# Pooled attention and a softplus feed-forward layer: two head pairs' attention results in one PSUM buffer, and the weights' combinations begun at the fifth chunk

## The chip, the cores and the metric

The kernel runs on one core of a Trainium2 chip. The metric is the device time of one execution in microseconds (us). The kernel before took 983.45 us (median of three runs, 981.61 to 985.9). Engines are named as the profile names them: PE is the matrix engine (PEld its weight loads), DVE is VectorE, ACT is ScalarE, POOL is GpSimd, SP is SyncE, which issues most of the DMAs.

## The reference

```python
# q, k, v: (8, 8, 576, 64) float32; w_in (512, 2048), w_out (2048, 512)
def _attn_ref(q, k, v):
    B, H, S, D = q.shape
    pool = 8
    Sp = S // pool                                   # 72 pooled keys
    k_p = k.reshape(B, H, Sp, pool, D).mean(axis=3)
    v_p = v.reshape(B, H, Sp, pool, D).mean(axis=3)
    scores = (1.0 / np.sqrt(D)) * np.matmul(q, k_p.transpose(0, 1, 3, 2))
    scores = scores - np.max(scores, axis=-1, keepdims=True)
    attn = np.exp(scores)
    attn = attn / (np.sum(attn, axis=-1, keepdims=True) + 1e-09)
    return np.matmul(attn, v_p)

def _moe_ref(x, w_in, w_out):                        # x: (4608, 512), the attention's output
    h = x @ w_in
    g = np.maximum(h, 0.0) + np.log1p(np.exp(-np.abs(h)))
    return g @ w_out
```

## The kernel before

**Chunks.** The 4608 tokens are cut into 18 chunks of 256 (two tiles of 128), numbered from 0. A batch has 576 tokens, so a chunk lies in one batch or spans two. For each chunk the kernel computes the attention, which gives the chunk's input x (512 wide, transposed, four head pairs m of 128 rows), then the first products (x with w_in), the softplus g, and the second products (g with w_out).

**High and low parts.** Every fp32 operand is split into a part rounded to the matmul's format and the rest of it, and a product is made of three matmuls: high with high, high with low, low with high. So each result that comes out of PSUM and goes into another matmul is read twice: ScalarE casts the high part, and VectorE subtracts it from the PSUM value for the low part. For the attention's result these two are `av_high` (line 500) and `av_low` (line 503), for the probabilities `PT_high` (432) and `PT_low` (437), for g `pair_softplus` (571) and `pair_low` (577).

**Two phases.** Chunks 0 to 2 and the attention of chunk 3 run in a first phase, while the weights are unpacked. All the rest is the second phase. There the first and second products go in pairs of feed-forward blocks, `u` = 0 to 7 for each chunk: `pair1` (24 matmuls of 256 columns, line 520) and, up to chunk 5, `pair2` (12 matmuls of 512, line 590). From chunk 6 on, `pair2_fast` (line 683) makes the second products with seven block products instead of eight, 21 matmuls of 256 columns. For that it needs sums of blocks of g (`sums`, `sums_high`, `sums_low`, lines 609, 614, 619) and combinations of blocks of w_out.

**The combinations of the weights** (`combine`, line 645; `combined_high`, 650; `combined_low`, 654; `put_t`, 658; `load_t`, 662) are made once, for each u: eight VectorE steps on 256 or 512 columns in two parts, and for each part a ScalarE cast, a VectorE subtraction and a store of 512 KB to DRAM. After chunk 5's products have released the weights that lie in their place, four loads of 256 KB for each u bring them back. They hold one of three `ld` buffers, which the loads of keys and values use too, and one of two `S` buffers per part.

**The order of the second phase** is a list made by a planner in the kernel's source (`Order`). Each operation has an engine, an estimated cost, the operations it waits for, and the buffers (`Slot`s) it holds. The planner walks through time; of the operations that an engine could start within 0.4 us of the earliest one, it takes the one with the highest rank (the estimated length of the work that hangs on it) plus a bonus `first`. `HURRY` is 60, `EARLY` is 100. The list fixes each engine's order; on the chip an engine takes its instructions in that order and waits where an input is late. Keys and values of the next batches go through SP (loads) and POOL (sums over eight rows).

**PSUM.** It has eight banks of 512 columns. In the second phase two are for first products, four for sums of second products, and two (`bank`) are for everything in the attention: transposes of q, scores, transposes of the probabilities, and the attention's results `avp`.

**Attention one chunk ahead.** In the stage of chunk c the attention of chunk c+1 goes on: transposes of q (`qTp`, 352), scores (365), their minimum and difference (373, 381), one exponential for the whole chunk (316) that waits for the third pair's softplus, sums and normalisation (396 to 412), transposes of the probabilities (`ptp`, 427, and `ltp`, 443), and at last `av_products` (497), for each head pair four matmuls of up to 256 columns for each batch in the chunk. Each head pair has a bank of its own turn: four matmuls (eight where the chunk spans two batches), one ACT cast and one DVE subtraction of 256 columns, and then the bank is free. The transposes of q for chunk c+2 need `av_products` of chunk c+1 and one of the two banks. The first step of first products of chunk c+1 is cut into 18 matmuls that need head pairs 0 to 2 and 6 that need head pair 3.

**Outputs.** Up to chunk 5, `output` copies the two sums out of their banks (ACT line 549, DVE line 551) with `HURRY`; later chunks are put together in `finish` (696, 704). The stores (`put`, 555) have no bonus and nothing hangs on them.

Of the kernel before, what the change touches and what calls it, by code (L numbers as in the profile page):

```python
# [9 lines left out]
F32 = mybir.dt.float32  # L10
# [84 lines left out]
def pooled_attention_softplus_ffn(  # L95
# [41 lines left out]
    def turn(banks, name):  # L137

        banks.append(banks.pop(0))
        return psum.tile([P, 512], F32, tag=banks[-1], name=name)  # L140
# [355 lines left out]
                                        (vsh[i][:, m], pl[:, m]), (vlo[i][:, m], lt[:, m // 2]))):  # L496
                nc.tensor.matmul(out=ps[:, r], lhsT=w, rhs=x[:, r], start=j == 0, stop=j == 3)  # L497

    def av_high(c, m, ps):
        nc.scalar.copy(out=pt_[c][0][:, m], in_=ps[:, 0:CT])  # L500

    def av_low(c, m, ps):
        nc.vector.tensor_tensor(out=pt_[c][1][:, m], in0=ps[:, 0:CT],  # L503
                                in1=pt_[c][0][:, m].bitcast(F32), op=ALU.subtract)

    def av(c, m):
        ps = turn(at_banks, "avp")
        av_products(c, m, ps)
        av_high(c, m, ps)
        av_low(c, m, ps)  # L510


    gs, accs = {}, {}
# [208 lines left out]
    def bank(s, name):  # L722
        if s.tile is None:
            s.tile = psum.tile([P, 512], F32, tag=s.name, name=name)
        return s.tile

    def act(n):
        return 0.14 + 0.00094 * n
# [447 lines left out]
    def probabilities(c, tiles, s_E, s_lt, subs):  # L1176
        s_x, norms, lows = x_slot[c], [], []
        parts = lambda n, k: [o for b in sorted({b for _, _, b in n}) for o in k.get(b, ())]
        ex = op(ACT, 1.2 + 2 * 1.28, lambda: exponential(e_[c]), [*subs, third[c - 1]], [s_E])
        for x in tiles:  # L1180
            s_sm, s_pm, s_pe = Slot("sm"), Slot("pm"), Slot("pe")
            o = op(DVE, 0.76, x.sum, [ex], [s_E, s_sm])
            o = op(DVE, 0.38, x.reciprocal, [o], [s_sm])
            m = op(DVE, 0.7, lambda x=x: x.main(nc.vector), [o], [s_E, s_sm, s_pm])
            e = op(DVE, 0.52, x.ends, [o], [s_E, s_sm, s_pe])
            s, r = Slot("bank"), Slot("bank")
            o = op(PE, 0.45, lambda x=x, s=s: x.PT(bank(s, "ptp")), [m], [s, s_pm], first=EARLY)
            h = op(ACT, act(512), lambda x=x, s=s: x.PT_high(s.tile), [o], [s, s_x])
            lows.append(op(DVE, dve2(512), lambda x=x, s=s: x.PT_low(s.tile), [h], [s, s_x]))
            o = op(PE, 0.15, lambda x=x, r=r: x.last(bank(r, "ltp")), [e], [r, s_pe], first=EARLY)  # L1190
            h = op(ACT, act(256), lambda x=x, r=r: x.last_high(r.tile), [o, h], [r, s_lt])
            lows.append(op(DVE, dve2(256), lambda x=x, r=r: x.last_low(r.tile), [h], [r, s_lt]))
        sp = spans(c * CT, (c + 1) * CT)
        for m in range(HP):
            s = Slot("bank")
            o = op(PE, 0.47 if len(sp) == 1 else 0.9,
                   lambda m=m, s=s: av_products(c, m, bank(s, "avp")),
                   [*lows, *parts(sp, v_ready)], [s, s_lt, s_x], first=EARLY)
            av_done[c].append(o)
            o = op(ACT, act(CT), lambda m=m, s=s: av_high(c, m, s.tile), [o], [s, s_x])  # L1200
            x_done[c].append(op(DVE, dve2(CT), lambda m=m, s=s: av_low(c, m, s.tile), [o],
                                [s, s_x]))

    def first_products(c, u, before):
# [7 lines left out]
        if u == 0:  # L1212
            wait += x_done[c] or [None]
        if u == 0:
            o = op(PE, 18 * MM, lambda: pair1(c, u, bank(s, "h"), range(KC - 1)), wait[:-1],
                   [s, x_slot[c]])
            o = p1[c, u] = op(PE, 6 * MM, lambda: pair1(c, u, s.tile, range(KC - 1, KC)),
                              [o, wait[-1]], [s, x_slot[c]])
        else:
            o = p1[c, u] = op(PE, 24 * MM, lambda: pair1(c, u, bank(s, "h")), wait,  # L1220
                              [s, x_slot[c]])
# [50 lines left out]
    def output(c, ends, banks):  # L1272
        s_o = [Slot("o") for _ in range(T)]
        if len(ends) > 1:
            s_u = Slot("u")
            o = op(ACT, 0.4, lambda: finish(c, 0), ends[:1], [*s_o, s_u, banks[0]], first=HURRY)
            i = op(DVE, 1.27, lambda: finish(c, 1), [o], [*s_o, s_u, *banks[:2]], first=HURRY)
            o = op(DVE, 1.7, lambda: finish(c, 2), [i, ends[1]], [*s_o, s_u, *banks[2:]],
                   first=HURRY)
            drained[c] = i, o  # L1280
            copies = [o] * T
        else:
            out_[c] = {}

            def copy(t):
                out_[c][t] = copy_out(c, t)
            copies = [op(DVE if t % 2 else ACT, 0.68, lambda t=t: copy(t), ends,
                         [s_o[t], banks[t]], first=HURRY) for t in range(T)]
        for t in range(T):
            op(SYNC, 1.0, lambda t=t: put(c, t, out_[c][t]), [copies[t]], [s_o[t]], lag=2.2)  # L1290

    def combinations():
        for u in range(FP):
            s_d, last, t_ready[u] = Slot("ld"), None, []
            for part in range(2):
                for step in range(4):
                    last = op(DVE, 0.7 if part == step == 0 else 0.43,
# [71 lines left out]
```

## Time and profile before

| | us |
|---|---|
| median of three runs | 983.45 |
| the profiled execution | 983.81 |
| its span, first to last instruction | 982.1 |
| PE busy | 942.4 |
| DVE busy | 669.0 |
| ACT busy | 420.6 |
| POOL busy | 117.6 |

The profile is of one execution. The granted PE clock over the whole span is 0.99 of full speed. Busy PE time is modelled and PE's instructions overlap; times of PE's wait rows (in square brackets behind an instruction, with what ended the wait) are idle time. The second phase begins at about 200 us; the stage of chunk 4 begins at 264.20 us, that of chunk 5 at 322.03, that of chunk 6 at 375.11, and from there on a stage takes about 51 us. The combinations run from 155.3 to 280.5 us, their reloads are issued from 324.6 to 380.1 us.

### The profile page before, as it was taken

What the parts mean: (1) busy time and instruction counts of PE and PEld (TensorE: products, weight loads), DVE (VectorE), ACT (ScalarE), POOL (GpSimd) and SP (SyncE); (2) the same over time, 40 slices, a digit from 0 to 9 for tenths busy, and PEclk for the clock granted to TensorE, in tenths of its full rate; (3) what the DMA queues carried; (4) which work ended last, traced back from release to release, by engine and by line L of the source; (5) the groups of instructions that cost most, each with busy time, mean ns of one, the idle gap of its engine ahead of it and who ended that gap; (6) DMA issues with size and microseconds to landing.
All of it is one profiled execution on the core that took longest, in us unless ns stands there. A gap on an engine that the chain in (4) does not pass through costs nothing.

```text
span 982.1 us, 18423 instructions
## 1 busy us (share of the span) xinstructions
PE 942.4 (96%) x7232; PEld 894.8 (91%) x7232; DVE 669.0 (68%) x1496; ACT 420.6 (43%) x854; POOL 117.6 (12%) x149
## 2 busy tenths in 40 slices
PE   5889999999899999999999999999999999999998
PEld 4679998898788899999999999999999999999997
DVE  5899987579874235767676766677757666666654
ACT  4763333444443333435353435353445343444332
POOL 1000001023342221042003300013200000000000
PEclk9999999999799999999999999999999999999999
DMA  9846343145262687578667847486747564755562
GB/s 252 262 154 236 126 153 139 58 157 179 78 208 55 183 251 248 188 227 240 185 196 202 260 146 224 151 241 193 244 140 236 162 214 153 214 173 194 172 213 88
DMA packets 105383, 181.56 MB, mean 185 GB/s; under 512 B 45648, under 2 KB 59984, under 8 KB 105296
## 3 DMA queue, kind: packets, MB, share of 16 engines
q1 hardware_dynamic: 103216, 179.86, 59.5%
q8 instruction: 57, 0.93, 0.4%
q10 hardware_dynamic: 2080, 0.52, 0.3%
q14 instruction: 30, 0.25, 0.1%
HBM read 154.14 MB, written 26.21 MB: 184 GB/s over the span
## 4 chain that ended last, share of the span: by engine, by line
PE 82%; DVE 11%; ACT 3%; DMA 2%; issue 1%; SPq 0%; DVEq 0%; ACTq 0%
PE h L520 38%; PE m L683 22%; PE acc L543 6%; PE acc L590 5%; PE sc L365 4%; PE avp L497 3%; PE qTp L352 2%; DVE sf L609 1%; PE ptp L427 1%; DVE d L645 1%; DVE t L654 1%; DVE xl L503 1%; DMA q<-in_q_dram 1%; ACT g L571 1%; DVE so L619 1%
## 5 line engine op out<-in xcount | busy, mean ns | idle before, releaser
L520 PE MATMUL h<-xh,w 128*128 128x256 f32 x2304 | 422.8, 284 | 2.4 <-DVE w L817 1.2
L520 PEld LDWEIGHTS h<-xh,w 128*128 128x128 f32 x2304 | 356.8, 189 | 6.7 <-DVE w L817 1.7
L520 PE MATMUL h<-xl,w 128*128 128x256 f32 x1152 | 324.6, 282 | 0.0
L571 ACT ACTIVATE g<-h 128x512 f32<-128x512 f32 x240 | 130.5, 596 | 292.5 <-PE h L520 278.3
L520 PEld LDWEIGHTS h<-xl,w 128*128 128x128 f32 x1152 | 217.4, 189 | 0.0
L683 PE MATMUL m<-w,so 128*128 128x256 f32 x1152 | 154.2, 282 | 0.0
L683 PEld LDWEIGHTS m<-w,so 128*128 128x128 f32 x1152 | 144.0, 188 | 0.0
L609 DVE TENSOR_TENSOR sf<-g 128x128 f32<-128x128 f32 x192 | 59.2, 308 | 119.5 <-ACT g L571 119.0
L683 PE MATMUL m<-w,g 128*128 128x256 f32 x576 | 113.4, 286 | 0.0
L577 DVE TENSOR_TENSOR gl<-g 128x512 fp32r<-128x512 f32 x120 | 85.6, 713 | 28.0 <-ACT g L571 28.0
L205 POOL TENSOR_TENSOR kst<-kst 72x512 f32<-72x512 f32 (+1 forms) x48 | 52.1, 1086 | 386.4 <-DMA kst<-in_k_dram 215.9
L683 PEld LDWEIGHTS m<-w,g 128*128 128x128 f32 x576 | 87.9, 188 | 0.0
L614 ACT CAST so<-sf 128x512 fp32r<-128x512 f32 x96 | 59.6, 621 | 57.5 <-DVE sf L609 57.5
L683 PE MATMUL m<-w,gl 128*128 128x256 f32 x288 | 80.9, 281 | 0.0
L619 DVE TENSOR_TENSOR so<-sf,so 128x512 fp32r<-128x512 f32 x96 | 69.3, 721 | 8.5 <-ACT so L614 1.6
L590 PE MATMUL acc<-w,g 128*128 128x512 f32 x192 | 63.0, 410 | 0.0
L373 DVE TENSOR_REDUCE mn<-sc 128x4 f32<-128x288 f32 x72 | 32.0, 453 | 42.5 <-PE sc L365 42.0
L543 PE MATMUL acc<-w,g 128*128 128x512 f32 x192 | 60.6, 396 | 0.3 <-ACT g L526 0.3
L526 ACT ACTIVATE g<-h 128x256 fp32r<-128x256 f32 (+1 forms) x96 | 31.9, 383 | 56.5 <-PE h L520 44.6
L683 PEld LDWEIGHTS m<-w,gl 128*128 128x128 f32 x288 | 54.2, 188 | 0.2 <-DVE gl L577 0.2
L365 PE MATMUL sc<-kbd,qT 128*128 128x144 f32 (+1 forms) x320 | 46.1, 297 | 1.9 <-DVE kbd L223 1.0
L365 PEld LDWEIGHTS sc<-kbd,qT 128*128 128x128 f32 (+1 forms) x320 | 38.8, 182 | 6.4 <-issue 1.7
(176 smaller groups left out, 1256.6 us busy)
## 6 DMA issues: line engine op xcount, KB each, us to landing
w<-wi SPq DMA_DIRECT2D x192, 512.0 KB
out_dram<-o SPq DMA_DIRECT2D x36, 256.0 KB
wst<-in_moe_w_in_dram SPq DMA_DIRECT2D x16, 512.0 KB
wst<-in_moe_w_out_dram SPq DMA_DIRECT2D x16, 512.0 KB
wi<-w SPq DMA_DIRECT2D x16, 512.0 KB
t<-t SPq DMA_DIRECT2D x16, 512.0 KB
w<-t SPq DMA_DIRECT2D x32, 256.0 KB
q<-in_q_dram SPq DMA_DIRECT2D x30, 256.0 KB
```

The source lines that it names most:

```text
L205: nc.gpsimd.tensor_tensor(out=out, in0=x, in1=y, op=ALU.add)
L365: nc.tensor.matmul(out=ps[r, (m % 2) * 2 * SP:(m % 2 + 1) * 2 * SP], lhsT=self.q[:, m, r], rhs=kbd[b % 2][:, m, :], start=True, stop=True)
L373: nc.vector.tensor_reduce(out=self.mn[:, 4 * i:4 * i + 4], in_=self.view(ps), axis=AX.X, op=ALU.min)
L520: nc.tensor.matmul(out=ps[:, 0:CT], lhsT=w[:, kc * P:(kc + 1) * P], rhs=x[:, kc], start=first and kc == j == 0, stop=last and kc == KC - 1 ...
L543: nc.tensor.matmul(out=accs[c][t], lhsT=a[:, ts], rhs=w, start=f == 0 and j == 0, stop=f == FC - 1 and j == 2)
L571: nc.scalar.activation(out=g, in_=ps.rearrange("p (k i) -> p k i", k=2), func=AF.Softplus)
L577: nc.vector.tensor_tensor(out=gl, in0=g, in1=gh.bitcast(F32), op=ALU.subtract)
L590: nc.tensor.matmul(out=accs[c][t], lhsT=a[:, k, ts], rhs=w, start=u == 0 and k == 0 and j == 0, stop=u == FP - 1 and k == 1 and j == 2)
L609: nc.vector.tensor_tensor(out=sf[:, o], in0=x, in1=y, op=how)
L614: nc.scalar.copy(out=so[:, 0], in_=ss[c, u])
L619: nc.vector.tensor_tensor(out=so[:, 1], in0=sf, in1=so[:, 0].bitcast(F32), op=ALU.subtract)
L683: nc.tensor.matmul(out=ms[c][n], lhsT=x, rhs=y, start=u == 0 and j == 0 and n in (1, 6, 5, 4), stop=u == FP - 1 and j == 2 and n in (2, 7, ...
```

## The change

Three things are changed, all in the second phase.

- The attention's results of two head pairs go into one bank, 256 columns each. They are one operation on PE, with estimated cost 0.94 (1.8 where the chunk spans two batches), and then one ACT cast and one DVE subtraction of 512 columns. The first step of a chunk's first products is cut in two halves of 12 matmuls: the first needs the first two head pairs, the second the other two.
- The first operation of each u's combinations waits for the first step of first products of chunk 4, `p1[NF - 2, 0]`, the fifth chunk; before, it waited for nothing.
- The copies of the sums of chunks 2 to 5, and all output stores, have a bonus of 2000 in place of 60 and 0.

```diff
-    def av_high(c, m, ps):
-        nc.scalar.copy(out=pt_[c][0][:, m], in_=ps[:, 0:CT])
-
-    def av_low(c, m, ps):
-        nc.vector.tensor_tensor(out=pt_[c][1][:, m], in0=ps[:, 0:CT],
-                                in1=pt_[c][0][:, m].bitcast(F32), op=ALU.subtract)
...
+    def av_high(c, m, ps, n=1):
+        nc.scalar.copy(out=pt_[c][0][:, m:m + n],
+                       in_=ps[:, 0:n * CT].rearrange("p (n i) -> p n i", n=n))
+
+    def av_low(c, m, ps, n=1):
+        nc.vector.tensor_tensor(out=pt_[c][1][:, m:m + n],
+                                in0=ps[:, 0:n * CT].rearrange("p (n i) -> p n i", n=n),
+                                in1=pt_[c][0][:, m:m + n].bitcast(F32), op=ALU.subtract)
...
-        for m in range(HP):
+        for m in range(0, HP, 2):
             s = Slot("bank")
-            o = op(PE, 0.47 if len(sp) == 1 else 0.9,
-                   lambda m=m, s=s: av_products(c, m, bank(s, "avp")),
-                   [*lows, *parts(sp, v_ready)], [s, s_lt, s_x], first=EARLY)
+
+            def products(m=m, s=s):
+                ps = bank(s, "avp")
+                for n in range(2):
+                    av_products(c, m + n, ps[:, n * CT:(n + 1) * CT])
+            o = op(PE, 0.94 if len(sp) == 1 else 1.8, products, [*lows, *parts(sp, v_ready)],
+                   [s, s_lt, s_x], first=EARLY)
             av_done[c].append(o)
-            o = op(ACT, act(CT), lambda m=m, s=s: av_high(c, m, s.tile), [o], [s, s_x])
-            x_done[c].append(op(DVE, dve2(CT), lambda m=m, s=s: av_low(c, m, s.tile), [o],
+            o = op(ACT, act(512), lambda m=m, s=s: av_high(c, m, s.tile, 2), [o], [s, s_x])
+            x_done[c].append(op(DVE, dve2(512), lambda m=m, s=s: av_low(c, m, s.tile, 2), [o],
                                 [s, s_x]))
...
-            o = op(PE, 18 * MM, lambda: pair1(c, u, bank(s, "h"), range(KC - 1)), wait[:-1],
+            o = op(PE, 12 * MM, lambda: pair1(c, u, bank(s, "h"), range(KC // 2)), wait[:-1],
                    [s, x_slot[c]])
-            o = p1[c, u] = op(PE, 6 * MM, lambda: pair1(c, u, s.tile, range(KC - 1, KC)),
+            o = p1[c, u] = op(PE, 12 * MM, lambda: pair1(c, u, s.tile, range(KC // 2, KC)),
                               [o, wait[-1]], [s, x_slot[c]])
...
-                         [s_o[t], banks[t]], first=HURRY) for t in range(T)]
+                         [s_o[t], banks[t]], first=2000) for t in range(T)]
         for t in range(T):
-            op(SYNC, 1.0, lambda t=t: put(c, t, out_[c][t]), [copies[t]], [s_o[t]], lag=2.2)
+            op(SYNC, 1.0, lambda t=t: put(c, t, out_[c][t]), [copies[t]], [s_o[t]], lag=2.2,
+               first=2000)
 
     def combinations():
         for u in range(FP):
-            s_d, last, t_ready[u] = Slot("ld"), None, []
+            s_d, last, t_ready[u] = Slot("ld"), p1[NF - 2, 0], []
```

More of the change, by code (lines that the diff above doesn't have):

```diff
@@ L497, in av_products @@
                 nc.tensor.matmul(out=ps[:, r], lhsT=w, rhs=x[:, r], start=j == 0, stop=j == 3)
-    def av_high(c, m, ps):
-        nc.scalar.copy(out=pt_[c][0][:, m], in_=ps[:, 0:CT])
-    def av_low(c, m, ps):
-        nc.vector.tensor_tensor(out=pt_[c][1][:, m], in0=ps[:, 0:CT],
-                                in1=pt_[c][0][:, m].bitcast(F32), op=ALU.subtract)
[L506 to L510, printed above, removed]
+    def av_high(c, m, ps, n=1):
[5 more added lines that the diff above has]
+                                in1=pt_[c][0][:, m:m + n].bitcast(F32), op=ALU.subtract)
     gs, accs = {}, {}
```

## The prediction

> **What bounds the kernel now.** I read the page first: busy times, then the chain of work that ended last.
>
> ```profile
> span 982.1 us, 18423 instructions
> ...
> PE 942.4 (96%) x7232; PEld 894.8 (91%) x7232; DVE 669.0 (68%) x1496; ACT 420.6 (43%) x854; POOL 117.6 (12%) x149
> ...
> PE 82%; DVE 11%; ACT 3%; DMA 2%; issue 1%; SPq 0%; DVEq 0%; ACTq 0%
> ```
>
> PE is busy for 96% and carries 82% of the chain; VectorE carries 11%. So work taken off VectorE or ScalarE pays only where PE stands idle for it. The change touches two such places: the stages in which the weights' combinations run, and the chunk boundaries, where the attention result of the next chunk is copied out of PSUM.
>
> For the first place I cut the time at the starts of first products (chunk 3, pair 1; chunk 4; chunk 5; chunk 6) and asked for busy time in these windows. The columns are the window, its length, PE, PE weight load, DVE, ACT and POOL busy with counts, granted clock, DMA share and GB/s.
>
> ```profile
> 206.19:264.20 58.01, 52.55 (x330) 46.92 (x329) 55.75 (x101) 25.08 (x45) 20.75 (x21) 0.93 0.46 151
> 264.20:322.03 57.83, 56.25 (x375) 50.43 (x374) 36.34 (x69) 22.26 (x40) 22.25 (x25) 0.98 0.41 119
> 322.03:375.11 53.08, 53.05 (x358) 48.62 (x358) 17.90 (x39) 17.89 (x32) 9.55 (x12) 1.00 0.79 232
> ```
>
> In the stage of chunk 3 VectorE is busy 55.75 of 58.01 us: there it is the bound, and PE is idle 58.01 - 52.55 = 5.46 us and runs at a granted clock of 0.93, which costs about 0.07 x 52.55 = 3.68 us. The stage of chunk 4 has 1.58 us of idle PE and 0.02 x 56.25 = 1.13 us of clock; the stage of chunk 5 has 0.03 us. The same windows for the combinations alone (tile d with its rounded tables t; columns DVE, ACT, clock, DMA share, GB/s), and PE's rows around the worst wait:
>
> ```profile
> 150.00:206.19 56.19, 4.24 (x9) 0.83 (x2) 1.00 0.27 91
> 206.19:264.20 58.01, 34.46 (x57) 7.15 (x12) 0.93 0.46 151
> 264.20:322.03 57.83, 8.68 (x15) 1.86 (x3) 0.98 0.41 119
> ```
>
> ```profile
> 250.79 1.12 PE L427 MATMUL ptp<-ident,pm 128*128 128x128 f32 x4 [3.31 <-DVE pm L405]
> ...
> 257.83 0.39 PE L443 MATMUL ltp<-ident,pe 128*96 128x128 f32 x2 [0.34 <-DVE lt__2751 L452]
> 258.89 0.33 PE L497 MATMUL avp<-xh,vsh 128*128 128x128 f32 x1 [0.67 <-DVE xl L437]
> ```
>
> ```profile
> 252.34 4.72 PE acc L590 x12
> ...
> 270.29 2.77 PE acc L590 x12
> ```
>
> Of VectorE's 55.75 us, 34.46 are combinations. The attention of chunk 4 is queued among them, its probabilities come late, PE waits 3.31 us, and twelve products just after take 4.72 us where twelve later ones take 2.77: the clock fell with that wait.
>
> For the second place, the waits of the whole run grouped by who waited for whom (us, times, longest):
>
> ```profile
> PE avp L497 <- DVE xl L503: 4.9, 9, 1.5
> ...
> PE ptp L427 <- DVE pm L405: 4.1, 2, 3.3
> ...
> PE qTp L352 <- DVE xl L503: 3.1, 7, 0.5
> ...
> PE ltp L443 <- DVE xl L437: 1.2, 2, 0.8
> ```
>
> The first and third, 8.0 us, are PE waiting until the low part of an attention result has been copied, so that one of the two attention banks comes free. One boundary in order of time:
>
> ```profile
> 467.94 0.28 PE L497 MATMUL avp<-xh,vsh 128*128 128x256 f32 x1
> ...
> 468.90 0.40 PE L683 MATMUL m<-w,g 128*128 128x256 f32 x2
> ...
> 469.11 0.65 ACT L500 CAST xh<-avp 128x256 fp32r<-128x256 f32 x2
> ...
> 471.34 0.76 DVE L503 TENSOR_TENSOR xl<-avp,xh 128x256 fp32r<-128x256 f32 x2
> 471.82 0.38 PE L497 MATMUL avp<-xh,vsh 128*128 128x256 f32 x1 [0.27 <-DVE xl L503]
> ...
> 473.48 1.14 PE L352 MATMUL qTp<-ident,q 128*128 128x128 f32 x8 [0.44 <-DVE xl L503]
> ...
> 474.37 0.48 PE L520 MATMUL h<-xh,w 128*128 128x256 f32 x2
> ```
>
> Head pairs 0 and 1 are multiplied from 467.94, then a step of second products fills in, and pairs 2 and 3 wait for the banks, then the next q transposes wait again; the first products of the new chunk start at 474.37.
>
> **The merge of two head pairs.** Fourteen chunks (4 to 17) go this way. Four ACT casts and four DVE subtractions of 256 columns become two each of 512. The old ones have their own groups; for the new ones the nearest are the copies of the probabilities, of the same kind and size:
>
> ```profile
> L503 DVE TENSOR_TENSOR xl<-avp,xh 128x256 fp32r<-128x256 f32 x72 | 28.8, 421 | 21.2 <-ACT xh L500 19.7
> L500 ACT CAST xh<-avp 128x256 fp32r<-128x256 f32 x72 | 25.9, 380 | 41.7 <-PE avp L497 40.2
> ...
> L437 DVE TENSOR_TENSOR xl<-ptp,xh 128x512 fp32r<-128x512 f32 x36 | 24.7, 687 | 3.9 <-ACT xh L432 3.4
> ...
> L432 ACT CAST xh<-ptp 128x512 fp32r<-128x512 f32 x36 | 21.3, 590 | 14.7 <-PE ptp L427 14.7
> ```
>
> Per chunk ACT saves 4 x 0.380 - 2 x 0.590 = 0.34 us and DVE 4 x 0.421 - 2 x 0.687 = 0.31, which by itself is off the path. What counts is the banks: two couples fit the two attention banks, so all four head pairs can be multiplied back to back (1.92 us, twice the 0.96 from 467.94 to 468.90), then the 2.5 us of second products run, and meanwhile both couples are copied. At the boundary shown, second products would end at 467.94 + 1.92 + 2.5 = 472.4. DVE is free for the couples at 471.34, as now: first low part done at 472.0, second at 472.7. The q transposes (0.89 us, 473.48 to 474.37) start at 472.4 and the first products at about 473.3 instead of 474.37. That is the 0.71 us of waits and a little more. Of the 8.0 us I take 6.0, since the second q transpose needs the second bank and where DVE is late some wait remains. Bounds: -8.0 and 0 (the list could keep the present order, and then the banks are reached no earlier).
>
> Two steps from the chain of waits give the size of what PE does in between, one of second and one of first products:
>
> ```profile
> 484.77 2.49 PE m L683 x21
> 487.26 2.84 PE h L520 x24
> ```
>
> The first part of a chunk's first step becomes 12 products instead of 18, about 12/24 x 2.84 = 1.42 us. The second couple's copy ends 0.69 us after the first, so that part hides it; with the cover gone it would cost 0.69 per chunk.
>
> [...] The trace shows the ACT copy at 469.11, behind both head pairs already, because softplus stands before it; by the row the sum keeps its -6.0.
>
> **The combinations begin with chunk 4.** Moved as one body: 64 DVE steps, 16 ACT casts, 16 DVE subtractions, 16 stores of 512 KB on SP; the 32 reloads of 256 KB stay tied to chunk 5's products. What this takes from the stage of chunk 3: 34.46 of 55.75 us of VectorE, so it is busy 21 of 58. The loss there is 5.46 + 3.68 = 9.14; I leave 0.34 + 0.67 of short waits and take -8.1. Bounds: -9.1 and -3.3 (only the long wait goes). On SP the stores no longer stand in front of the key and value loads of batch 2:
>
> ```profile
> SPq L658 <- DVE t L654: 40.2, 11, 9.7
> ```
>
> That helps the same stage and is inside its 9.14.
>
> What it brings to the stages of chunks 4 and 5: 34.46 + 8.68 + 4.24 = 47.4 us of VectorE. In chunk 4 the rest of VectorE is 36.34 - 8.68 = 27.7 us, so 30.2 fit and 17.2 go on into chunk 5, where 35 are idle. So chunk 4's stage becomes as full as chunk 3's is now, and the first combination waits at the head of DVE's queue for PE's first step of chunk 4, with splits and attention queued behind it. What differs is the slack: chunk 4's values were finished at the last moment before its first products, while chunk 5's are copied early:
>
> ```profile
> 307.20 0.90 DVE L503 TENSOR_TENSOR xl<-avp,xh 128x256 fp32r<-128x256 f32 x2 [1.00 <-ACT xh L500]
> ...
> 322.03 2.84 PE h L520 x24
> ```
>
> 14 us lie between. But PE takes its list in order, so a late transpose stops it all the same. The trace shows no such stage; bounds: nothing (-2.7, also the present waits and the carried clock go), or all 47.4 us at chunk 3's rate, 47.4 / 34.46 x 9.14 = 12.6, less 2.7: +9.9. I take one stall like the 3.31 and two like the present ones of this stage (4.1 - 3.3 = 0.8, and 0.8), 4.9, less 2.7: +2.2.
>
> **Stores ahead.** For chunks 2 to 5 the copies of the sums, and for all chunks the stores, go first:
>
> ```profile
> 206.49 0.60 ACT L549 COPY o<-acc 128x512 f32<-128x512 f32 x1
> ...
> 280.44 1.27 DVE L551 COPY o<-acc 128x512 f32<-128x512 f32 x2
> ```
>
> Chunk 2's second half sits in its bank until 280 now. Four chunks have four banks, so nobody waited; zero. Against it: 0.69 us of DVE ahead of a split at four stage ends, at most +2.8. On SP a store now waits for its copy with loads behind it; the loads' slack covers a microsecond.
>
> **Sum.** 983.81 (span 982.1 and 1.7 around it) - 6.0 - 8.1 + 2.2 + 0 = 971.9. The profiled execution is 0.36 above the median of 983.45, so 971.5.
>
> **Rivals.** *The stall moves whole.* VectorE next to POOL is slow wherever it is:
>
> ```profile
> 274.91 3.81 DVE L645 TENSOR_TENSOR d<-d,w 128x256 f32<-128x256 f32 x5
> ...
> 275.59 2.23 POOL L205 TENSOR_TENSOR kst<-kst 72x512 f32<-72x512 f32 x2 [6.62 <-DMA kst<-in_k_dram]
> ```
>
> 0.76 us per step here, where the group's mean is 0.47; and POOL is busy 22.25 us in chunk 4's stage, 20.75 in chunk 3's. Then chunk 4's stage pays the +9.9: 971.5 + 7.7 = 979.2, or 985.2 if the boundaries gain nothing as well. For it: the fullness. Against: 14 us of slack and 17 us that spill into an easy stage. [...]
>
> *The combinations hide.* -2.7 in place of +2.2: 966.6. For it: the spare VectorE time over both stages, 110.9 - 93.0 = 17.9 us.
>
> *The merge doesn't do what it says*: banks are met in the old order. 971.5 + 6.0 = 977.5.
>
> *Slower: attention slips by a step.* With copies later, the next q transposes may fall behind a further PE step, and scores with them. The exponential has this slack in a fast stage:
>
> ```profile
> 438.10 0.81 DVE L381 TENSOR_TENSOR E<-sc,mn 128x288 f32<-128x288 f32 x2
> ...
> 442.40 1.28 ACT L316 ACT_TABLE_LOAD   x1
> ```
>
> 3.5 us from the scores' end (438.9) to its table load. A slip beyond that moves the exponential behind the next softplus, the values end a step late, and PE has only one step (2.49 us) to put in between: about 2.5 us at each of eleven boundaries, 27, so 971.5 + 6.0 + 27 = 1005. Against it: one slipped step of 2.8 us stays under 3.5.
>
> **Chances.** Forecast 0.46; hidden 0.14; merge without effect 0.12; stall moved 0.19; slip 0.09. A difference under 0.5% (4.9 us) can't be told from none: faster is below 978.5, slower above 988.4. Faster: 0.46 + 0.14 + 0.07 + 0.05 = 0.72; same: 0.05 + 0.13 = 0.18; slower 0.10 (the slip and a little of the moved stall). The range, 963 to 984, leaves out the slip and the two ends; the likeliest case alone spans 967 to 977.
>
> **What would show it.** Right: DVE near 22 us busy and the clock at 1.00 in the stage before chunk 4, which takes some 50 us; no wait of PE on L427 there; PE's two waits on the attention copies (8.0 us) near 2; combinations from about 255 to 340 us. Wrong: a wait over 3 us with a fallen clock in chunk 4's or 5's stage (stall moved); head pairs still apart around the second products (merge); q transposes one step later in the fast stages, and waits on the attention copies above 8 us (slip); PE waiting for the reloaded tables at chunk 6 would be a case that I left out.

## The result, and the profile after

The changed kernel takes 975.41 us (median of eight runs, 972.38 to 979.31), against 982.83 for the kernel before in the same session: a ratio of 0.9924, 95% interval 0.9901 to 0.9948. The forecast was 971.5 with a range of 963 to 984; its likeliest case reached from 967 to 977. The profiled execution took 975.02 us. The medians below leave out two runs in a slow state (1157.5 us, of the kernel with the merge and the combinations, and 3218.84 us, of the kernel before).

The low part of the attention's result is now line 504 (503 before); behind it, line numbers after the change are smaller by four: first products 516 (520), second products 586 and 679 (590 and 683), the combinations 641 (645), the stores and reloads of the tables 654 and 658, and the copies and stores of the sums 545, 547 and 551. Kernels below that keep the head pairs apart have the old numbers, and the two that change POOL's sums have numbers smaller by two more.

The page of the changed kernel:

```profile
span 972.9 us, 18364 instructions
...
PE 937.9 (96%) x7232; PEld 892.0 (92%) x7232; DVE 668.1 (69%) x1468; ACT 417.4 (43%) x826; POOL 119.1 (12%) x149
...
PE 81%; DVE 11%; ACT 4%; issue 2%; DMA 1%; DVEq 0%; ACTq 0%
```

VectorE's share of the chain is what it was, 11%. The stages of chunks 3, 4 and 5 again, from first products to first products; columns as in the prediction (window, length, PE, weight load, DVE, ACT, POOL, granted clock, DMA share, GB/s):

```profile
208.95:259.01 50.06, 48.80 (x331) 44.30 (x330) 21.80 (x42) 17.57 (x31) 20.53 (x24) 1.00 0.30 75
259.01:316.32 57.31, 54.77 (x374) 49.34 (x374) 51.92 (x100) 25.46 (x45) 17.31 (x18) 1.00 0.46 142
316.32:369.06 52.74, 52.74 (x358) 48.45 (x358) 33.64 (x68) 21.04 (x35) 2.99 (x3) 1.00 0.77 248
```

The same windows for the combinations alone:

```profile
259.01:316.32 57.31, 27.11 (x48) 5.58 (x9) 1.00 0.46 142
316.32:369.06 52.74, 17.50 (x33) 4.34 (x7) 1.00 0.77 248
```

Chunk 3's stage went from 58.01 to 50.06 us, at full clock, with VectorE 21.80 us busy. Chunks 4 and 5 together went from 110.91 to 110.05, though 44.61 us of combinations now stand in them. The time before chunk 3's stage grew from 206.19 to 208.95, and what follows chunk 5's stage shrank from 982.1 - 375.11 = 606.99 to 972.9 - 369.06 = 603.84. So the span's -9.2 is +2.76 - 7.95 - 0.86 - 3.15.

PE's waits in the whole run:

```profile
PE ptp L427 <- DVE xl L437: 2.8, 2, 2.5
PE ptp L427 <- DVE pm L405: 2.7, 3, 1.1
...
PE qTp L352 <- DVE xl L504: 1.8, 3, 1.1
PE m L679 <- DVE o L700: 1.4, 2, 0.7
```

The 8.0 us of waits on attention copies are down to 1.8. The third row is all that is left of them. A boundary in order of time, the one shown in the prediction:

```profile
461.05 0.28 PE L497 MATMUL avp<-xh,vsh 128*128 128x256 f32 x1
...
461.91 2.22 POOL L205 TENSOR_TENSOR kst<-kst 72x512 f32<-72x512 f32 x2 [20.05 <-DMA kst<-in_k_dram]
...
462.21 1.26 DVE L605 TENSOR_TENSOR sf<-sf,g 128x128 f32<-128x128 f32 x1
...
462.96 0.40 PE L679 MATMUL m<-w,g 128*128 128x256 f32 x2
...
465.98 1.29 DVE L504 TENSOR_TENSOR xl<-avp,xh 128x512 fp32r<-128x512 f32 x2
466.73 1.25 PE L352 MATMUL qTp<-ident,q 128*128 128x128 f32 x8 [1.12 <-DVE xl L504]
```

All four head pairs are multiplied back to back from 461.05 to 462.96, and second products follow without a wait, as forecast. Then PE waits 1.12 us for the low parts, because POOL starts its adds at 461.91 and a VectorE step that takes 0.29 us elsewhere takes 1.26.

### The profile page after: what moved, and what is told of

It reads as the page before. It is cut to its first block, busy times and chain, and to the rows that moved or that the text cites. A ratio compares the mean times of both kernels' runs of the same rounds, so it can differ in the third digit from the quotient of the medians.

```text
span 972.9 us, 18364 instructions
## 1 busy us (share of the span) xinstructions
PE 937.9 (96%) x7232; PEld 892.0 (92%) x7232; DVE 668.1 (69%) x1468; ACT 417.4 (43%) x826; POOL 119.1 (12%) x149
## 4 chain that ended last, share of the span: by engine, by line
PE 81%; DVE 11%; ACT 4%; issue 2%; DMA 1%; DVEq 0%; ACTq 0%
PE h L516 37%; PE m L679 21%; PE acc L539 6%; PE acc L586 5%; PE sc L365 4%; PE avp L497 3%; DVE sf L605 2%; PE qTp L352 1%; PE ptp L427 1%; DVE d L641 1%; DVE so L615 1%; DVE gl L573 1%; DMA q<-in_q_dram 1%; DVE pm L405 1%; DVE o L700 1%
## 5 line engine op out<-in xcount | busy, mean ns | idle before, releaser
L615 DVE TENSOR_TENSOR so<-sf,so 128x512 fp32r<-128x512 f32 x96 | 72.0, 750 | 7.6 <-ACT so L610 0.9
L539 PE MATMUL acc<-w,g 128*128 128x512 f32 x192 | 60.6, 396 | 0.4 <-ACT g L522 0.4
```

Of the source, the lines that this page charges most:

```text
L539: nc.tensor.matmul(out=accs[c][t], lhsT=a[:, ts], rhs=w, start=f == 0 and j == 0, stop=f == FC - 1 and j == 2)
L615: nc.vector.tensor_tensor(out=so[:, 1], in0=sf, in1=so[:, 0].bitcast(F32), op=ALU.subtract)
```

## The experiments

Eight kernels make a full table of the three parts (the kernel before, the change, each part alone and each pair). Differences are (ratio - 1) x 983 us against the kernel before on the same chip. The stage columns are worked out from each profile's PE rows: the time at which the first phase's second products end, the lengths from there to the end of chunk 3's, 4's and 5's second products, and the rest of the span.

| kernel | median | ratio (95%) | difference | first phase | chunk 3 | chunk 4 | chunk 5 | rest |
|---|---|---|---|---|---|---|---|---|
| before | 981.3 to 983.2 | 1 | | 206.3 | 66.7 | 54.6 | 53.1 | 601.3 |
| merge | 976.97 | 0.9932 (0.9906 to 0.9959) | -6.7 | 207.6 | 63.4 | 54.3 | 52.7 | 597.1 |
| combinations | 997.98 | 1.0164 (1.0130 to 1.0198) | +16.1 | 207.9 | 60.6 | 59.9 | 53.1 | 616.8 |
| stores | 989.46 | 1.0070 (1.0040 to 1.0099) | +6.9 | 207.3 | 72.8 | 53.7 | 53.0 | 601.2 |
| merge, combinations | 989.05 | 1.0060 (1.0036 to 1.0084) | +5.9 | 207.0 | 57.2 | 54.6 | 52.8 | 612.6 |
| combinations, stores | 985.81 | 1.0032 (1.0010 to 1.0053) | +3.1 | 208.9 | 58.1 | 55.5 | 53.1 | 605.3 |
| merge, stores | 984.98 | 1.0019 (1.0001 to 1.0037) | +1.9 | 207.5 | 72.3 | 53.0 | 52.7 | 595.5 |
| the change | 975.41 | 0.9924 (0.9901 to 0.9948) | -7.5 | 209.1 | 57.5 | 55.4 | 52.7 | 598.2 |

The merge gains in all four settings: 6.7 alone, 16.1 - 5.9 = 10.2 with the combinations, 6.9 - 1.9 = 5.0 with the stores, 3.1 + 7.5 = 10.6 with both. The other two parts each lose without the other: the combinations moved cost 16.1 or 12.6 us without the stores ahead, and gain 3.8 or 9.4 with them; the stores ahead cost 6.9 or 8.6 without the combinations moved, and are worth 13.0 or 13.4 with them.

Taken together, these two parts cost 3.1 us without the merge, and with it they bring 0.8 us (7.5 against 6.7), where the intervals of the two kernels overlap almost wholly. So the table does not show that the change is faster than the merge alone.

### Each part alone

The merge alone is the diff that is shown above without its last part (two head pairs in one bank, 12 and 12 products).

> The kernel before with the merge of two head pairs alone (with the 12/12 split of a chunk's first step). Theory (the parts add up): PE's waits on the attention copies fall from 8.0 us to about 2, new waits behind a slow VectorE take a part back, and the time falls by 3 us, 2 to 4, as the changed kernel gained 3.15 us from chunk 6 to the end; the stage of chunk 3 still loses some 9 us. Rival (only together): without the combinations out of the way VectorE is late for the couples, nothing gained, 0 to -1. Rival (the merge is all of the gain): -7.

Measured: -6.7 us, close to the -7 of the rival that gives the whole gain to the merge, and not the -2 to -4 of parts that add up. In the profiles 4.2 lie behind chunk 5 (601.3 to 597.1) and 3.3 in chunk 3's stage. The boundaries are worth less than the -6.0 of the prediction. The 3.3 are for the most part the clock: PE's idle time in that stage is 5.15 us against 5.46, but 3.41 us of the stage ran at half clock (granted 0.50) against 10.24 in the kernel before. With half of PE's busy time in them as an estimate of the loss, that is 1.7 against 4.5 us.

The combinations alone:

```diff
-            s_d, last, t_ready[u] = Slot("ld"), None, []
+            s_d, last, t_ready[u] = Slot("ld"), p1[NF - 2, 0], []
```

> The kernel before with only the combinations begun at chunk 4. Theory (the parts add up): the stage of chunk 3 takes 50 us in place of 58, the stages of chunks 4 and 5 together 110 to 111 as before, from chunk 6 on as before; -5 to -8 us. Rival (the stall moves, and only the merge or the early stores kept it small in the changed kernel): the stage of chunk 4 takes 62 us or more, and the whole gains 0 to -3.

Measured: +16.1. Chunk 3's stage gains 6.1, chunk 4's loses 5.3 to a wait of 4.05 us on the transposes of the probabilities and 6.83 us at half clock around its end, and the rest loses 15.5. Its order of time in chunk 6's first stage:

```profile
387.29 3.78 SPq L266 DMA_DIRECT2D kst<-in_k_dram  x1
391.11 8.21 SPq L555 DMA_DIRECT2D out_dram<-o  x5
395.44 0.69 DVE L551 COPY o<-acc 128x512 f32<-128x512 f32 x1 [7.98 <-DMA out_dram<-o]
396.06 0.58 ACT L549 COPY o<-acc 128x512 f32<-128x512 f32 x1 [9.32 <-DMA out_dram<-o]
...
396.24 2.90 PE L683 MATMUL m<-w,so 128*128 128x256 f32 x12 [11.25 <-issue]
```

PE waits 11.25 us. I first read this as a wait for the reloaded tables, since a reload is issued late too, and the expectation of a later run says so. The rows show another chain: without a bonus, five stores of sums stand in SP's list behind the reloads and behind a key load that itself takes 3.78 us to issue; the `o` buffers stay held, the copies of chunk 5's sums wait 7.98 and 9.32 us for them, and PE needs the banks that those copies free. For this last step the profile names no releaser; the first of the copies ends at 396.13, and PE goes on at 396.24. In the kernel before, with the same lack of bonus, the four stores of chunks 4 and 5 were issued between 360.2 and 384.1.

The stores ahead alone:

```diff
-                         [s_o[t], banks[t]], first=HURRY) for t in range(T)]
+                         [s_o[t], banks[t]], first=2000) for t in range(T)]
...
-            op(SYNC, 1.0, lambda t=t: put(c, t, out_[c][t]), [copies[t]], [s_o[t]], lag=2.2)
+            op(SYNC, 1.0, lambda t=t: put(c, t, out_[c][t]), [copies[t]], [s_o[t]], lag=2.2,
+               first=2000)
```

> The kernel before with only the copies of the sums and the output stores ahead. Theory (the parts add up): no difference, within 2 us; the second half of chunk 2's sums is copied near 210 us and not at 280, and nobody had waited for it. Rival (SP's order is what counts): stores that stand earlier let loads of keys pass, -3 or more; or stores wait for their copies in front of the loads, +3 or more.

Measured: +6.9, all of it in chunk 3's stage (66.7 to 72.8). Two rows of the kernel before, in order of time:

```profile
202.44 0.35 SPq L266 DMA_DIRECT2D kst<-in_k_dram  x1
206.67 2.45 POOL L205 TENSOR_TENSOR kst<-kst 72x512 f32<-72x512 f32 x2 [36.41 <-DMA kst<-in_k_dram]
```

and with the stores ahead:

```profile
207.60 0.84 SPq L555 DMA_DIRECT2D out_dram<-o  x2
208.53 0.38 SPq L266 DMA_DIRECT2D kst<-in_k_dram  x1
...
212.35 2.15 POOL L205 TENSOR_TENSOR kst<-kst 72x512 f32<-72x512 f32 x2 [41.14 <-DMA kst<-in_k_dram]
...
255.61 0.86 DVE L300 TENSOR_SCALAR lt<-vl,lmask 32x128 f32<-32x128 f32 x4 [2.74 <-POOL vl L205]
...
258.99 1.09 PE L427 MATMUL ptp<-ident,pm 128*128 128x128 f32 x4 [5.75 <-DVE xl L437]
```

The store of chunk 2's sums waits on SP for their copies, with the first key load of batch 2 behind it. The load goes from 202.44 to 208.53, POOL's first sum from 206.67 to 212.35, and so on down the row of loads and sums; VectorE waits 2.74 us at 255.61 for POOL's last value sum, and behind that wait in its queue stand the second half of the probabilities and the low part that PE waits 5.75 us for. The stage in one row (columns as above):

```profile
207.30:280.00 72.70, 62.59 (x381) 56.96 (x380) 60.60 (x118) 28.81 (x52) 26.10 (x27) 0.86 0.49 157
```

PE is idle for 10.11 us of it, against 5.46 before; and 20.48 us of it ran at half clock, against 10.24.

### The pairs

> The merge and the combinations from chunk 4, without the stores ahead. Alone the merge gave 6.2 us, the combinations lost 14.8 and the stores lost 6.3, all three together gave 7.4: 22.1 us are not the sum of the parts. Theory 'the stores ahead are what lets the combinations end in time': then this kernel keeps the wait for the reloaded tables in chunk 6's first stage (some 10 us and a fallen clock) and comes out near 983 - 6 + 15 = 992. Rival 'the merge is what does it, since it empties VectorE and ScalarE in the attention': then the wait is gone without the stores, and the time is that of all three, 975 to 978.

Measured: +5.9, a wait of 10.85 us in chunk 6's first stage, and five stores issued together at 380.5. This is the theory's outcome, the merge does not cure it; only the name that the expectation gives the wait is wrong.

> The combinations from chunk 4 and the stores ahead, head pairs apart as before. Theory 'stores ahead let the combinations end in time': the wait for the reloaded tables at chunk 6 is gone, the stages from chunk 6 on take the 601 us of before, chunk 3's stage keeps its gain of 6 to 8, so 977 to 982. Rival 'the merge does it': the wait for the tables stays, and the time is 998 + 6 = 1004, or 998 if the two losses do not add.

Measured: +3.1. The long wait is gone, chunk 3's stage keeps its gain (58.1), chunk 4's has one wait of 2.12 us; so the stores ahead are what lets the combinations move. But the time is above the 977 to 982 of the theory, because the rest is 605.3 and not 601.

> The merge and the stores ahead, the combinations where they were. If the parts add here: 983.2 - 6.2 + 6.3 = 983, with chunk 3's stage near 69 us by PE's ends (it was 66.7 before, 72.8 with the stores ahead alone, 63.4 with the merge alone). Rival 'the loss of the stores alone was the two head-pair copies queued behind the sums' copies, and the merge leaves one fewer of each to queue': chunk 3's stage stays at 63, and the time is that of the merge alone, 977.

Measured: +1.9, chunk 3's stage 72.3 with waits of 5.47 and 2.28 us: the loss of the stores stays as it was, and the parts add. The stage does not come down to the 69 that the expectation added up, since the merge's 3.3 there were mostly the clock, and 20.48 us run at half clock here as with the stores alone.

### What the stores' two halves do

Stores ahead, copies with their old bonus (the change but for one line):

```diff
-                         [s_o[t], banks[t]], first=2000) for t in range(T)]
+                         [s_o[t], banks[t]], first=HURRY) for t in range(T)]
```

> The change, but the copies of the sums keep their old bonus of 60; only the stores stand ahead in the list. In the kernels with the combinations moved and no stores ahead, five stores of sums were issued together at 380 to 399 us, behind the reloads of the tables and a key load; the copies of chunk 5's sums waited for the o buffers that those stores held, and PE waited some 11 us for the banks that these copies free. Theory 'the place of the stores on SP is what counts': here the stores are early, there is no such wait, and the time is that of the change, 975 to 978. Rival 'it is the copies' own bonus': the copies come late on VectorE as without the change, a wait of several us stays in chunk 6's first stage, 983 to 990.

Measured: 974.11 us, ratio 0.9918 (0.9903 to 0.9933); no long wait. So the place of the stores on SP is what counts, and the copies' bonus is worth nothing that can be measured. This version is as fast as the change or a little faster; the two intervals overlap.

The stores ahead alone, but not chunk 2's:

```diff
-               first=2000)
+               first=2000 if c > 2 else 0)
```

> The stores ahead alone (that kernel took 989.5), but the store of chunk 2's sums keeps its old place. Theory 'SP stood waiting for chunk 2's sums with the key loads of batch 2 behind it (the load went from 202.4 to 208.5 us), and POOL's sums, the low parts of the values and the probabilities followed six us late': here the load is back at about 202.5, the wait of 5.7 us on the transposes of the probabilities is gone, and the time is 983, that of the kernel before. Rival 'the 0.69 us copies of the sums stand ahead of the splits on VectorE': the wait stays, 988 to 990.

Measured: 982.74 us, ratio 1.0003 (0.9985 to 1.0020). The first key load is back at 202.02 us and the wait of 5.75 is one of 3.03, as in the kernel before (3.31). That one store, ahead of the key loads, was the whole loss.

### Where the combinations begin

Spread over chunks 4 and 5, one start for each u:

```diff
-            s_d, last, t_ready[u] = Slot("ld"), p1[NF - 2, 0], []
+            s_d, last, t_ready[u] = Slot("ld"), p1[NF - 2 + u // 4, 2 * (u % 4)], []
```

> The changed kernel, but the eight combinations are let go one by one: u waits for chunk 4's steps 0, 2, 4, 6 and then chunk 5's steps 0, 2, 4, 6. Theory (what is left in chunk 4's stage is VectorE's fullness): VectorE in that stage falls from 52 to some 45 us, the wait of 2.54 us on the transposes there goes or halves, and the time falls by 1 to 3 us against the changed kernel, so -8 to -11 against before. Rival (POOL beside VectorE makes that wait, whatever the fullness): the wait stays, no difference from the changed kernel, -7 against before. Rival (reloads become late): PE waits for the reloaded tables in chunk 6's stage, slower than the changed kernel by 3 us or more.

Measured: 985.53 us, ratio 1.0024 (1.0003 to 1.0046). Chunk 4's stage is at 54.3 its longest wait now 1.0 us, as the first theory said, but chunk 6 waits again. In order of time:

```profile
379.87 0.90 SPq L654 DMA_DIRECT2D t<-t  x2
...
386.05 0.62 ACT L610 CAST so<-sf 128x512 fp32r<-128x512 f32 x1 [5.46 <-DMA t<-t]
...
386.72 3.23 PE L679 MATMUL m<-w,so 128*128 128x256 f32 x12 [6.55 <-ACT so L610]
```

The last tables are stored at 379.87. Until the stores land, both `S` buffers are held, and chunk 6's sums of g (`so`) need one: PE waits 6.55 us. This is the outcome of the third theory, slower by more than 3 us, with a wait for a buffer in place of the reloaded tables: the other end of the room for the combinations.

Earlier, from chunk 3's sixth pair on:

```diff
-            s_d, last, t_ready[u] = Slot("ld"), p1[NF - 2, 0], []
+            s_d, last, t_ready[u] = Slot("ld"), p1[NF - 3, 5], []
```

> The change, but the combinations begin with the sixth pair of chunk 3 (five of its eight steps done) instead of with chunk 4. Theory 'VectorE has room at the end of chunk 3's stage (it is busy 21.8 of 50.1 us there) and too much to do in chunk 4's (51.9 of 57.3)': some 8 us of combinations move forward, chunk 4's stage loses its waits of about 2.5 us, 972 to 974. Rival 'the end of chunk 3's stage is where the probabilities of chunk 4 go through VectorE, and the combinations stand in front of them again': a wait on the transposes of the probabilities of 2 to 4 us at about 250 us, 977 to 982.

Measured: 980.36 us, ratio 0.9979 (0.9963 to 0.9994), five us worse than the change. Chunk 3's stage is 60.9 by PE's ends, chunk 4's 57.7. The costliest wait, in order of time:

```profile
284.09 2.17 POOL L205 TENSOR_TENSOR vst<-vst 128x512 f32<-128x512 f32 x2 [4.83 <-DMA vst<-in_v_dram]
284.25 2.91 DVE L641 TENSOR_TENSOR d<-d,w 128x256 f32<-128x256 f32 x3
...
290.28 0.66 PE L427 MATMUL ptp<-ident,pm 128*128 128x128 f32 x4 [3.33 <-DVE pm L405]
```

Three combination steps beside POOL take 0.97 us each in place of 0.42, with chunk 5's probabilities behind them, and PE waits 3.33 us; the three steps' stretch is 1.65 us of that. The size is what the rival said, the place is not: the wait came at 290 us in chunk 4's stage, not at 250.

### VectorE beside POOL

The change, with POOL's two larger adds left out for batches 2 to 7; only the last add, of two partial rows, is made, so the key and value sums are over two rows and not eight. The order of the work is the same.

```diff
-        for out, x, y in ((t[:, :, 0:4], t[:, :, 0:4], t[:, :, 4:8]),
-                          (t[:, :, 0:2], t[:, :, 0:2], t[:, :, 2:4]),
-                          (o, t[:, :, 0], t[:, :, 1])):
+        for out, x, y in ((o, t[:, :, 0], t[:, :, 1]),):
```

> The change with POOL's two larger adds of every key and value sum of batches 2 to 7 left out (the sums are then over too few rows; the last add stays). The order of the work is the same. Theory 'what is left of PE's waits in chunk 4's stage and at the boundaries comes from VectorE slowed while POOL adds': combination steps near 0.42 us throughout chunk 4's stage, PE's waits after 160 us fall from 13.6 to below 6, and the time is 966 to 970. Rival 'these waits come from the order of the work, POOL only happens to be there': waits above 10 us stay, 973 to 975.

Measured: 964.12 us, ratio 0.9809 (0.9788 to 0.9829), 11.3 us below the change. PE's waits from 376 us on, of the kernel before, with the change, and without most of POOL's adds:

```profile
PE avp L497 <- DVE xl L503: 4.7, 8, 1.5
PE qTp L352 <- DVE xl L503: 3.1, 7, 0.5
PE ptp L427 <- DVE xl L437: 1.7, 2, 1.3
```

```profile
PE ptp L427 <- DVE pm L405: 2.7, 3, 1.1
PE qTp L352 <- DVE xl L504: 1.8, 3, 1.1
PE m L679 <- DVE o L700: 1.4, 2, 0.7
```

```profile
PE sc L363 <- ACT qT L357: 1.6, 7, 0.2
```

Every wait on VectorE in the fast stages is gone. The same instruction in the change and without POOL's adds (count; shortest, median and longest in ns; first and last start):

```profile
L641 DVE TENSOR_TENSOR d<-d,w x40: 418/425/944, 269.4 to 332.6; 128x256 f32<-128x256 f32 x40
```

```profile
L639 DVE TENSOR_TENSOR d<-d,w x40: 409/425/428, 270.2 to 331.1; 128x256 f32<-128x256 f32 x40
```

The median is the same; only the steps beside POOL are long. The theory holds, and its gain was set too small. By PE's ends 9.4 us lie behind chunk 5 (598.2 to 588.8), 2.8 in chunk 4's stage (55.4 to 52.6) and 3.6 in the first phase (209.1 to 205.5), while chunk 3's stage lost 4.8 for a reason of its own (last section). Of the 9.4, the rows account for 5.3 (6.9 us of listed waits against 1.6); the other 4.1 no row explains. Another reading would be that VectorE does not run slower but waits for POOL's late sums. Behind chunk 5 of the change it does so once (3.30 us at 434.44, through ScalarE's part of the values), and no wait of PE above 0.25 us stands near it.

The sums on VectorE instead, on top of the kernel with the copies' old bonus:

```diff
+        nc.vector.tensor_reduce(out=o, in_=t.rearrange("p a s d -> p a d s"), op=ALU.add,
+                                axis=AX.X)
...
-            prev = op(POOLE, 2.5, lambda i=i: x["k_pool"](i), [o], [s, s_kp])
+            prev = op(DVE, 1.2, lambda i=i: x["k_pool"](i), [o], [s, s_kp])
```

(likewise for the values; three adds on POOL fall away, and the planner's lag of these loads is 4.5 in place of 2.4).

> The change with the copies' old bonus (974.1 us), and the sums over eight rows of keys and values of batches 2 to 7 made by VectorE, one reduction of 1024 columns each in place of POOL's three adds; the planner's cost of one is 1.2 us, and the lag of their loads 4.5 us in place of 2.4. Without most of POOL's adds the time was 964.1. A reduction of 576 columns takes 748 ns, so one of 1024 some 1.3 us, 42 of them 55 us on VectorE, against 109 POOL rows of up to 1.5 us that slow what stands beside them. Theory 'VectorE has the room, and what counts is that nothing runs beside it': PE's waits at the boundaries fall below 5 us in all, 967 to 972. Rival 'the reductions stand in VectorE's queue in front of splits and wait there for loads': new waits on the probabilities and attention copies, 975 to 982.

Measured: 982.84 us, ratio 1.0004 (0.9990 to 1.0018). PE's longest wait of that kernel, and one of the reductions:

```profile
PE m L677 <- ACT so L608: 9.4, 1, 9.4
```

```profile
L202 DVE TENSOR_REDUCE kp<-kst x24: 1950/1990/2006, 208.1 to 735.8; 72x128 f32<-72x1024 f32 x24
```

The time is above the 975 to 982 of the rival, and the long wait is not one that it named. A reduction takes 1.99 us, not the 1.3 I had scaled from a row of 576. The waits on VectorE at the boundaries are gone here too, but the reductions push the combinations back in chunks 4 and 5, the last table is stored at 383 us, and chunk 6's sums wait 9.39 us for an `S` buffer, as in the spread kernel; chunk 3's stage (65.4) has its stall back. The gain that lies in POOL's adds is real, and this way of getting it spends it.

## Why the prediction was right, and where it was not

**The time** (971.5 forecast, 975.41 measured) is inside the likeliest case's range, and that is partly luck. The forecast sum was -11.9 us, the span changed by -9.2. By stages only one of the four terms is nearly exact, that of chunk 3's stage; the boundaries gained 2.85 us less than forecast and chunks 4 and 5 cost 3.06 less, which cancels, and the 2.76 of the first phase were in no term. By parts the sum was further off: the merge alone gives -6.7, and the other two, forecast at -5.9 together, add 0.8 to it.

**The merge** was forecast at -6.0 from the boundaries. What it does there is as described, head pairs back to back and 8.0 us of waits down to 1.8. But the term is mis-sized: behind chunk 5 the change gains 3.15 us, the merge alone 4.2. What failed is to take each microsecond of those waits for a gain. They fell by 6.0 in the fast stages, with 1.8 left where the forecast had 2; but 2.7 + 1.4 us of others came up, on the probabilities and on the finished sums, where the run without POOL's adds has none. All listed waits there fell only from 9.5 to 6.9. POOL's work there grew as well, from 58.3 to 71.1 us busy behind chunk 5, while it fell from 20.75 + 22.25 + 9.55 to 20.53 + 17.31 + 2.99 in the three stages before: keys and values of later batches are summed later. The kernel with combinations and stores but no merge shows that price without the cover: its rest is 605.3, against 601.3 before (of the 4.0, PE's idle time is 2.3, and a fall of the clock to half over 3.41 us costs up to 1.7, an estimate from the two). Over the whole run the merge is still worth 5.0 to 10.6 us; with the combinations moved it also takes chunk 4's stage from 59.9 to 54.6. The case "the merge does nothing" is out. So is "attention slips by a step", which was to be seen as waits above 8 us on the attention copies. The prediction kept the -6.0 by a row in which the copy starts behind both head pairs, since a softplus stands before it. In the change it is the same: the couple's copy is one instruction that reads both head pairs, so it could not start before the second pair's products in any case; at the boundary above these are over at about 462.2, and ScalarE, busy with a softplus until then, starts the copy at 462.25.

**Chunk 3's stage** was forecast at -8.1 and measured at -7.95, with the marks that were named: about 50 us, VectorE at 21.8, clock 1.00, only 0.26 us of waits on the transposes of the probabilities. The side remark on SP, that the tables' stores no longer stand before batch 2's loads, was half of the truth: the store of chunk 2's sums now does, and the first key load is issued at 210.24 us in place of 202.44. With the combinations gone from this stage VectorE has the slack to bear it. How near the two numbers are is in part luck with the clock: the same order of work without POOL's adds lost 4.8 us in this stage to a fall of it (last section), and of the eight runs of the change, with granted clocks from 0.990 to 0.998, the profiled one is one of the two at 0.998.

**The stages of chunks 4 and 5** were forecast at +2.2 and measured at -0.86. "One stall like the 3.31" came as one wait of 2.54 us (in the row of 2.8 above), and it is all of PE's idle time in these two stages, where the forecast had 4.9 us of waits; 2.54 less the 2.7 that went is close to what was measured. The clock stayed at 1.00 after that wait. The forecast had put no price on a fall there, though the 3.31 in the kernel before had one beside it. The combinations ran from 262 to 357 us, not to 340.

**Stores ahead** is the step that failed: "four chunks have four banks, so nobody waited; zero", with a bound of +2.8. Alone they cost 6.9 us, and with the combinations moved they are worth 13. Both signs come from SP, of which the prediction said "a store now waits for its copy with loads behind it; the loads' slack covers a microsecond". It was six microseconds in front of batch 2's loads, and there the slack was none as long as the combinations filled VectorE. The other side, that combinations moved alone would leave the stores behind the reloads with `o` buffers and banks held, I did not see at all: I costed the move of the combinations as if the order on SP stayed. Of the case named as left out, PE waiting at chunk 6, the wait is real in the kernels without stores ahead, though it is for a bank and not for the reloaded tables. So the parts cannot be read as a sum: -6.7 + 16.1 + 6.9 would be +16.3, and together they are -7.5.

**The first phase** took 2.76 us more in the profiled execution and was not in the sum. In the other profiles its end lies between 205.5 and 208.9; the version with the copies' old bonus, whose first phase holds the same work, has 206.7. So it looks like a difference from one execution to the next, which one profile for each kernel doesn't settle.

**The rivals.** "The stall moves whole" was written for +9.9 in chunk 4's stage, and the change doesn't show it. Its mechanism is there, in the combinations alone (4.05 us, stage +5.3) and in the kernel that starts in chunk 3 (3.33 us): it decides as soon as the combinations' steps, POOL's adds and the probabilities meet. The other side, that the combinations hide, is nearer to what came: -0.86, forecast -2.7. The row on which "the stall moves whole" rests, 0.76 us for a combination step beside POOL against a mean of 0.47, has its like in the change: up to 944 ns against a median of 425 for the same instruction, and nothing above 428 for it once POOL's larger adds are gone.

## What to carry to other kernels

When one part of a change moves a block of work in a planned list, follow every queue past which its neighbours slide, the store queue first: a store that waits for its data holds up each load behind it (here the first key load went from 202.44 to 208.53 us), and a store put last holds buffers that stop the matrix engine several steps away (here for 11.25 us). Parts that lose alone can gain together, so measure pairs before dropping one, and set the whole against its best part alone: here the merge alone came within 0.8 us of all three. When VectorE's waits move about without end, look for what runs beside it: leaving out one engine's work for a single run shows how much is there to gain (here 11.3 us).

## What the runs showed of the hardware

One of VectorE's combination steps (`d<-d,w`, with two inputs in SBUF) took up to 944 ns beside POOL's adds in the change, more than twice its median of 425; a step of the sums of g (`sf<-sf,g`), also with two, took 1.26 us in place of 0.29. The subtractions of attention results, with one of their two inputs in PSUM, did not stretch: of the 72 in the kernel before, five of which ran beside an add, none took over 426 ns, at a median of 424. So "VectorE next to POOL is slow wherever it is", as the prediction has it, is too wide. In chunk 4's stage and behind chunk 5, 12.2 us of the changed kernel's time went with those adds. A reduction of 1024 elements that are read 256 bytes apart took 1.99 us, against 748 ns for 576 that lie in a row: 1.94 ns an element against 1.30.

The granted clock did not follow the length of a single wait. Without POOL's adds, waits of 0.26, 0.53 and 0.47 us among the transposes at 249 to 251 us were followed by 10.24 us at half clock (granted 0.50); in the change the same three waits (0.26, 0.53 and 0.47, at 252 to 255) were not, nor was the single one of 2.54. First without POOL's adds, then the change (columns as above):

```profile
242.00:252.00 10.00, 8.73 (x57) 7.32 (x56) 7.14 (x19) 4.02 (x8) 1.32 (x3) 0.99 0.01 2
252.00:262.00 10.00, 10.00 (x49) 10.00 (x49) 1.38 (x2) 1.76 (x3) 0.00 (x0) 0.50 0.00 0
```

```profile
245.00:255.00 10.00, 8.74 (x55) 7.20 (x55) 9.31 (x21) 4.22 (x9) 4.31 (x5) 1.00 0.01 2
255.00:265.00 10.00, 10.00 (x82) 9.74 (x82) 4.56 (x9) 3.34 (x6) 1.33 (x3) 1.00 0.29 62
```

That is the 4.8 us that chunk 3's stage lost there. The falls of the clock that begin and end inside the program last 3.41 us or twice that in the kernel before (17.51 to 20.92, 34.57 to 37.99, 249.61 to 256.44, 263.27 to 266.68) and 3.41 in the change (36.29 to 39.70); the other times at half clock, 10.24 us without POOL's adds, 6.83 and 13.65 with the combinations alone, 20.48 with the stores ahead, are multiples of 3.41 as well. In the kernel before the starts also lie multiples of it apart (17.07, 215.04 and 13.65 us). Idle time of PE just before a fall does not tell these stretches from others. In the 3.41 us before one, PE was busy for 1.29 in the kernel before (246.20 to 249.61), for 1.88 in the kernel that starts in chunk 3 (257.16 to 260.57) and for 2.15 without POOL's adds (248.42 to 251.84), while in the change, counted in steps of 3.41 from its own fall, stretches with 1.69 (288.88 to 292.29) and 2.17 (251.33 to 254.74) passed without a fall. So in these runs idle time alone does not decide it; what does was not tried.
